# Pooled attention and a SiLU layer: the first batch's values loaded in two halves that are added by DMA, and its queries transposed earlier

## The chip, the cores and the metric

The kernel runs on one core of one Trainium2 chip. The metric is the device time of one execution in microseconds, the median of several runs. The profile is one execution taken by the hardware profiler; its times are counted from the start of its span. The engines are PE (TensorE: products, with PEld for its weight loads), DVE (VectorE), ACT (ScalarE), POOL (GpSimd) and SP (SyncE). DMA transfers are issued from the queues of POOL, SP and ACT and move on 16 DMA engines.

## The reference

```python
B, H, S, D = 8, 8, 576, 64           # batch, heads, sequence, head width
k_p = k.reshape(B, H, S // 8, 8, D).mean(axis=3)      # 72 pooled keys
v_p = v.reshape(B, H, S // 8, 8, D).mean(axis=3)      # 72 pooled values
scores = matmul(q, k_p.T) / sqrt(D)
attn = exp(scores - max) ; attn /= attn.sum(-1) + 1e-9
x = (attn @ v_p)  -> [B * S, H * D] = [4608, 512]
h = x @ w_in                          # 512 -> 2048
out = (h * sigmoid(h)) @ w_out        # 2048 -> 512, float32
```

Eight neighbouring keys, and eight neighbouring values, are averaged; attention runs against the 72 averages; its output goes through a layer with SiLU.

## The kernel before

The tokens go through the layer in nine tiles of 512 (t = 0 to 8), and attention of batch t + 1 is woven into tile t. Only batch 0 has nothing to hide behind: its attention is the head of the program.

In the head, keys and values are laid out with one group of eight rows (8 x 64 numbers) per partition: 576 groups make 4.5 slots of 128 partitions. A slot group is folded in three additions on VectorE (512 to 256 to 128 to 64 numbers per slot); products with a shifted identity ("select") then bring the sums into the order that attention needs.

```python
SLOTS, SA = 4, 3                       # four full slots and half a slot; tiles of 3 and 2 slots
RE = POOL * D                          # 512 numbers: eight rows

def load_slots(eng, b, name, i0, i1, half=None):
    es = slice(0, RE) if half is None else slice(half * RE // 2, (half + 1) * RE // 2)
    ...
    how = dict(accum_op=ALU.add) if half else {}      # half 1 is added to what half 0 left
    ...
    eng.dma_start(out=tiles[j][..., :w], in_=src[...], **how)

def slot_sums(name, j, halves=False):
    raw = row_tiles[name][j]
    dst = rows5[name][:, SA:] if j else rows5[name][:, :SA]
    w = RE // 4 if halves else RE // 2                # halves: one fold less
    while w > D:
        nc.vector.tensor_add(out=raw[..., :w], in0=raw[..., :w], in1=raw[..., w : 2 * w])
        w //= 2
    nc.vector.tensor_add(out=dst, in0=raw[..., :D], in1=raw[..., D : 2 * D])
```

`q_transpose(b, a, f)` is one VectorE transpose of a quarter of a batch's queries; `scores(b, g, f)` are eight products and four exponentials on ScalarE; `denominators` are four products and a reciprocal; `numerators(b, g, f)` are eight products with the pooled values and two multiplications on VectorE that write `xT`, the input of the layer. `warm_up(n)` issues n products whose result nobody uses.

The head of the program:

```python
    ... keys of batch 0 on the SP and ACT queues ...
    load_q(0, halves=True)
    load_q_half(0, 0)
    load_slots(nc.gpsimd, 0, "v", 0, 3)
    load_q_half(0, 1)
    load_slots(nc.gpsimd, 0, "v", 3, 4)
    load_slots(nc.gpsimd, 0, "v", 4, 5)
    attn_tables()
    nc.vector.memset(warm, 0.0)
    nc.vector.memset(ones, float(POOL))
    nc.gpsimd.memset(shifts, 0.0)
    make_identity(nc, ident, nomemset=True)
    # ... cut ...
    for c in range(3):
        load_w_in(512 * c, 512 * (c + 1))             # on the GpSimd queue, two transfers each

    warm_up(19)
    slot_sums("k", 0)
    select_k(0, 0)
    copy_k(0, 0, act_copy)
    warm_up(4)
    q_transpose(0, 0, 0)
    scores(0, 0, 0)
    slot_sums("k", 1)
    warm_up(3)
    select_k(0, 1)
    copy_k(0, 1, act_copy)
    q_transpose(0, 1, 0)
    warm_up(2)
    scores(0, 1, 0)
    denominators(0, 0, 0)
    slot_sums("v", 0)
    warm_up(2)
    select_v(0, 0, "mm")
    copy_v(0, 0, act_copy)
    denominators(0, 1, 0)
    q_transpose(0, 0, 1)
    scores(0, 0, 1)
    slot_sums("v", 1)
    warm_up(1)
    numerators(0, 0, 0, ("mm", "at"))
    warm_up(2)
    select_v(0, 1, "mm")
    copy_v(0, 1)
    q_transpose(0, 1, 1)
    warm_up(2)
    numerators(0, 1, 0, ("mm", "at"))
    scores(0, 1, 1)
    warm_up(2)
    ... keys, queries and values of batch 1, the last of w_in, and w_out on the GpSimd queue ...
    for t in range(NT):
        ...
        up(t, f_up, items)             # x @ w_in, SiLU
        ...                            # down: @ w_out
```

The first real products of the layer are those of `up(0, ...)`, line 518 of the kernel before; its first columns need both `numerators` groups of the head. Batch 2's keys and values are already loaded in halves by this kernel (`load_half_2`, during t = 0).

Of the kernel before, what the change touches and what calls it, by code (L numbers as in the profile page):

```python
# [36 lines left out]
def kernel(  # L37
# [9 lines left out]
    nc = tc.nc  # L47
# [185 lines left out]
    SLOTS = ROWS // 128  # L233
# [5 lines left out]
    SA = SLOTS - 1  # L239
# [10 lines left out]
    def load_slots(eng, b, name, i0, i1, half=None):  # L250
        es = slice(0, RE) if half is None else slice(half * RE // 2, (half + 1) * RE // 2)
        src = (k if name == "k" else v)[b].rearrange("h (sp p) d -> (h sp) (p d)", p=POOL)
        src = src[:, es]
        how = dict(accum_op=ALU.add) if half else {}
        tiles = row_tiles[name]
        w = es.stop - es.start
        if i0 == SLOTS:
            eng.dma_start(
                out=tiles[1][:REST, SLOTS - SA, :w], in_=src[128 * SLOTS :], **how
            )  # L260
        else:
            j = i0 // SA
            eng.dma_start(
                out=tiles[j][:, i0 - SA * j : i1 - SA * j, :w],
                in_=src[128 * i0 : 128 * i1].rearrange("(i r) e -> r i e", r=128), **how
            )

    def slot_sums(name, j, halves=False):
        raw = row_tiles[name][j]
        dst = rows5[name][:, SA:] if j else rows5[name][:, :SA]  # L270
        w = RE // 4 if halves else RE // 2
        while w > D:
            nc.vector.tensor_add(  # L273
                out=raw[..., :w], in0=raw[..., :w], in1=raw[..., w : 2 * w]
            )
            w //= 2
        nc.vector.tensor_add(out=dst, in0=raw[..., :D], in1=raw[..., D : 2 * D])
# [40 lines left out]
    def copy_v(b, a, copy=nc.vector.tensor_copy):  # L318
        hs = slice(4 * a, 4 * (a + 1))
        copy(out=batches[b]["vp"][:, hs, :], in_=batches[b]["v_ps"][:SP, hs, :])  # L320
# [3 lines left out]
    def scores(b, g, f):  # L324
        st = batches[b]
        sc = [ps_tile([128, 512], FP32, "at", "sc_ps")[:SP, :HS] for s in range(4)]
        for c in range(2):
            for s in range(4):
                rows = slice(32 * s, 32 * (s + 1))
                nc.tensor.matmul(  # L330
                    sc[s],
                    lhsT=kz[b % 2][rows, g, c, :],
                    rhs=st["qT"][rows, g, f * QF : (f + 1) * QF, c, :],
                    start=(c == 0), stop=(c == 1),
                )
        es = mid.tile([SP, 4, HS], BF16, tag="es", bufs=4, name="es")
        for s in range(4):
            nc.scalar.activation(es[:, s, :], sc[s], func=AF.Exp, scale=score_scale)  # L338
        st[f"es{g}{f}"] = es


    def denominators(b, g, f, on_dve=False):
        st = batches[b]
        es = st[f"es{g}{f}"]
        den_ps = ps_tile([128, 512], FP32, "at", "den_ps")
        for s in range(4):
            nc.tensor.matmul(  # L347
                den_ps[32 * s : 32 * (s + 1), :HS],
                lhsT=ones, rhs=es[:, s, :], start=True, stop=True,
            )  # L350
        rec = mid.tile([128, HS], FP32, tag="rec", bufs=4, name="rec")
        if on_dve:
            nc.vector.reciprocal(rec, den_ps[:, :HS])
        else:
            lnd = mid.tile([128, HS], FP32, tag="lnd", name="lnd")
            nc.scalar.activation(lnd, den_ps[:, :HS], func=AF.Ln)  # L356
            nc.scalar.activation(rec, lnd, func=AF.Exp, scale=-1.0)
        st[f"rec{g}{f}"] = rec
# [318 lines left out]
    load_slots(nc.sync, 0, "k", 4, 5)  # L677
    load_q(0, halves=True)
    load_q_half(0, 0)
    load_slots(nc.gpsimd, 0, "v", 0, 3)  # L680
    load_q_half(0, 1)
    load_slots(nc.gpsimd, 0, "v", 3, 4)
    load_slots(nc.gpsimd, 0, "v", 4, 5)
    attn_tables()
    nc.vector.memset(warm, 0.0)
    nc.vector.memset(ones, float(POOL))
# [12 lines left out]
    def load_w_out(c):  # L699
        cs = slice(c * KG // 4, (c + 1) * KG // 4)  # L700
        nc.gpsimd.dma_start(out=w_out_sb[:, cs, :], in_=w_out_r[:, cs, :])

    for c in range(3):
        load_w_in(512 * c, 512 * (c + 1))

# [12 lines left out]
    q_transpose(0, 1, 0)  # L718
    warm_up(2)
    scores(0, 1, 0)  # L720
    denominators(0, 0, 0)
    slot_sums("v", 0)
    warm_up(2)
    select_v(0, 0, "mm")
    copy_v(0, 0, act_copy)
    denominators(0, 1, 0)
    q_transpose(0, 0, 1)
    scores(0, 0, 1)
    slot_sums("v", 1)
    warm_up(1)  # L730
    numerators(0, 0, 0, ("mm", "at"))
    warm_up(2)
    select_v(0, 1, "mm")
    copy_v(0, 1)
    q_transpose(0, 1, 1)
    warm_up(2)
    numerators(0, 1, 0, ("mm", "at"))
    scores(0, 1, 1)
    warm_up(2)
# [8 lines left out]
    load_slots(nc.gpsimd, 1, "v", 3, 4)  # L748
    load_slots(nc.gpsimd, 1, "v", 4, 5)
    load_w_out(3)  # L750

    def load_half_2(name, half):
        for i0, i1 in ((0, SA), (SA, SLOTS), (SLOTS, SLOTS + 1)):
            load_slots(nc.gpsimd, 2, name, i0, i1, half)

    visits = [(f, g) for f in range(2) for g in range(2)]
    for t in range(NT):
# [42 lines left out]
        if a < B:  # L800
            q_at = [15, 16, 17, 49] if t > 1 else [24, 25, 26, 49] if t else [82, 84, 86, 88]
            if t == 0:
                for j in range(2):
                    f_up.append((44 + 8 * j, lambda j=j: slot_sums("k", j)))
                    f_up.append((72 + 8 * j, lambda j=j: select_k(1, j)))
                    f_up.append((72 + 8 * j, lambda j=j: copy_k(1, j)))
                    f_down.append((20 + 10 * j, lambda j=j: slot_sums("v", j)))
                    f_down.append((37 + 3 * j, lambda j=j: select_v(1, j, "at")))
                    f_down.append((37 + 3 * j, lambda j=j: copy_v(1, j)))
            elif t == 1:  # L810
                for j in range(2):
                    f_up.append((0, lambda j=j: slot_sums("k", j, halves=True)))
                    f_up.append((22, lambda j=j: select_k(2, j)))
                    f_up.append((23, lambda j=j: copy_k(2, j)))
                    f_down.append((8, lambda j=j: slot_sums("v", j, halves=True)))
                    f_down.append((40, lambda j=j: select_v(2, j, "at")))
                    f_down.append((41, lambda j=j: copy_v(2, j)))
            else:
                f_up.append((22, lambda: k_transpose(a)))
                f_down.append((10, lambda: pool_v(a)))  # L820
            for n in range(4):
                f_to = f_down if t and n == 3 else f_up
                f_to.append((q_at[n], lambda n=n: q_transpose(a, n // 2, n % 2)))
            if t == 0:
                f_down.append((0, lambda: load_half_2("k", 0)))
                f_down.append((0, lambda: load_q(2)))
                f_down.append((0, lambda: load_half_2("k", 1)))
                for half in range(2):
                    f_down.append((31, lambda half=half: load_half_2("v", half)))
                for y in range(2):  # L830
                    for n in U_W:
                        f_down.append((6, lambda y=y, n=n: unit_weight_sum(y, n)))
            elif a + 1 < B:
                for stage in range(2):
                    f_down.append((100, lambda stage=stage: pool_k(a + 1, stage)))
                f_up.append((0, lambda: load_q(a + 1)))
                f_up.append((1, lambda: load_one(a + 1, "k")))
                f_up.append((2, lambda: load_rest(a + 1, "k")))
                f_down.append((11, lambda: load_one(a + 1, "v")))
                f_down.append((12, lambda: load_rest(a + 1, "v")))  # L840
            f_down.append((0, attn_tables))

            if t:
                sc_at, den_at, nu_at = (1, 28, 56, 77), (28, 46, 69, 89), (46, 69, 89, 93)
            else:
                sc_at, den_at, nu_at = (1, 14, 22, 30), (14, 22, 30, 38), (42, 47, 52, 57)
            for n, (f, g) in enumerate(visits):
                f_down.append((den_at[n], lambda f=f, g=g: denominators(a, g, f)))
                f_down.append((sc_at[n], lambda f=f, g=g: scores(a, g, f)))


            for n, (f, g) in enumerate(visits):
                if n < 3 or not 3 <= t < B - 2:
                    at = nu_at[n] + 2 * (t == 1 and n == 0)
                    f_down.append((at, lambda f=f, g=g: numerators(a, g, f)))
                if n == 0 and 3 < t < B - 1:
                    f_down.append((nu_at[n], lambda: numerators(a - 1, 1, 1)))
# [34 lines left out]
```

The softmax here doesn't subtract the row's maximum and nothing guards it: scores larger than these inputs give would overflow.

## Time and profile before

| | |
|---|---|
| device time, median of 3 | 291.53 us (291.43 to 291.8) |
| span of the profiled execution | 288.6 us |
| granted TensorE clock | 0.998 |
| DMA | 37.67 MB, mean 131 GB/s |
| busy in the first 23 us: PE / DVE / ACT / POOL | 20.38 / 17.39 / 12.35 / 15.05 us |

A row of the timeline has the start in us, the duration in us, the engine, the line of the kernel, the operation with its output and input, and the count of merged instructions; a bracket gives how long the engine had been idle before and what it was waiting for. "PE busy" counts warm-up products too. A row of DMA issues has the count, the size and the microseconds from issue to landing. A row of the table by stretches has, after the engines, the granted clock, the DMA share and the GB/s moved.

### The profile page before, as it was taken

The numbers are of one execution on the slowest core, as the hardware profiler recorded it, in microseconds if no ns is written. First come the engines' busy times: TensorE is split into PE (matmuls) and PEld (weight loads), VectorE is DVE, ScalarE is ACT, GpSimd is POOL, SyncE is SP. The second block draws the span as 40 slices with busy tenths as digits, with TensorE's granted clock in tenths as the row PEclk, the third lists the DMA queues.
The fourth block names the chain that finished last, engine by engine and source line by source line (L and its number), as shares of the span: only waits on it lengthen the run. The fifth ranks groups of instructions, "written<-read, shape, count | busy, mean of one in ns | idle before, by whom it ended". The sixth has DMA issues, their size and how long they took to land.

```text
span 288.6 us, 6600 instructions
## 1 busy us (share of the span) xinstructions
PE 281.2 (97%) x2578; PEld 189.9 (66%) x2597; DVE 226.8 (79%) x417; ACT 187.9 (65%) x401; POOL 52.2 (18%) x68
## 2 busy tenths in 40 slices
PE   7989999999999999999999999999999999999995
PEld 2448434465667676657788767676777667786684
DVE  4986844989789796979698879887988876746783
ACT  1768675568656877578767866786679657425700
POOL 8744316501020011101200106203000000000000
PEclk9999999999999999999999999999999999999999
DMA  7999999893758565875995495979830023005004
GB/s 214 276 278 215 232 301 151 221 206 55 145 82 187 127 91 76 133 179 123 137 182 166 61 138 81 164 156 163 149 82 2 2 65 83 1 2 140 6 2 145
DMA packets 35295, 37.67 MB, mean 131 GB/s; under 512 B 9952, under 2 KB 27616, under 8 KB 35264
## 3 DMA queue, kind: packets, MB, share of 16 engines
q0 software_dynamic: 21760, 20.86, 43.3%
q1 hardware_dynamic: 12928, 15.48, 22.0%
q10 hardware_dynamic: 576, 0.92, 0.9%
q8 instruction: 20, 0.33, 0.5%
q14 instruction: 11, 0.09, 0.1%
HBM read 36.70 MB, written 9.44 MB: 160 GB/s over the span
## 4 chain that ended last, share of the span: by engine, by line
PE 91%; DVE 2%; ACT 2%; DMA 2%; issue 1%; DVEq 0%
PE hp_ps L518 24%; PE o_psP L623 15%; PE o_psQ L623 15%; PE u_psQ L460 6%; PE u_psP L460 6%; PE o_psR L623 5%; PE o_ps L550 4%; PE sc_ps L330 4%; PE nu_ps L370 3%; PE den_ps L347 3%; PE u_psR L460 2%; DMA raw<-in_k_dram 2%; PE warm_ps L672 1%; ACT es L338 1%; PE kz_ps L295 1%
## 5 line engine op out<-in xcount | busy, mean ns | idle before, releaser
L518 PE MATMUL hp_ps<-xT,w_in_sb 128*128 128x512 bf16 (+3 forms) x398 | 80.5, 338 | 1.2 <-ACT h_T L524 0.4
L524 ACT ACTIVATE h_T<-hp_ps 128x512 bf16<-128x512 f32 (+2 forms) x95 | 51.4, 545 | 33.1 <-PE hp_ps L518 31.9
L623 PEld LDWEIGHTS <-h_sum 128*128 128x128 bf16 x640 | 60.4, 98 | 15.2 <-issue 6.1
L583 DVE TENSOR_TENSOR h_sum<-h_T 128x1024 bf16<-128x1024 bf16 (+1 forms) x72 | 50.9, 743 | 7.0 <-ACT h_T L524 7.0
L518 PEld LDWEIGHTS <-w_in_sb 128*128 128x128 bf16 x412 | 39.3, 98 | 24.9 <-issue 1.5
L338 ACT ACTIVATE es<-sc_ps 72x288 bf16<-72x288 f32 x128 | 41.4, 402 | 12.6 <-PE sc_ps L330 12.5
L378 DVE TENSOR_TENSOR xT<-nu_ps,rec 128x288 bf16<-128x288 f32 x64 | 25.8, 450 | 13.2 <-PE nu_ps L370 13.0
L460 PEld LDWEIGHTS <-w_sum 128*128 128x128 bf16 x300 | 29.3, 98 | 7.7
L623 PEld LDWEIGHTS <-h_T 128*128 128x128 bf16 x256 | 23.5, 98 | 6.7 <-issue 4.3
L468 ACT ACTIVATE h_T<-c_sb 128x512 bf16<-128x512 f32 x30 | 18.8, 628 | 10.8 <-DVE c_sb L492 10.8
L152 DVE STREAM_TRANSPOSE qT<-q_bf 128x576 bf16<-128x576 bf16 x32 | 22.9, 753 | 0.0
L181 POOL DMA_DIRECT2D raw<-in_k_dram x5 | 7.0, 1405 | 75.1 <-DVE h_sum L583 37.7
L356 ACT ACTIVATE lnd<-den_ps 128x288 f32<-128x288 f32 x30 | 12.3, 411 | 10.8 <-PE nu_ps L370 5.8
L273 DVE TENSOR_TENSOR raw<-raw 128x384 f32<-128x384 f32 (+3 forms) x20 | 12.4, 619 | 8.0 <-DMA raw<-in_v_dram 4.4
L623 PE MATMUL o_psP<-w_out_sb,h_sum 128*128 128x256 bf16 x128 | 17.6, 273 | 0.0
L623 PE MATMUL o_psQ<-w_out_sb,h_sum 128*128 128x256 bf16 x128 | 17.6, 273 | 0.0
L623 PE MATMUL o_psQ<-w_sum,h_T 128*128 128x256 bf16 x128 | 17.5, 274 | 0.0
L623 PE MATMUL o_psP<-w_sum,h_sum 128*128 128x256 bf16 x128 | 17.0, 273 | 0.0
L623 PE MATMUL o_psR<-w_sum,h_sum 128*128 128x256 bf16 x128 | 16.7, 273 | 0.0
L623 PE MATMUL o_psP<-w_sum,h_T 128*128 128x256 bf16 x128 | 16.7, 273 | 0.0
L530 POOL DMA_DIRECT2D out_dram<-o_sb x1 | 0.6, 628 | 82.3 <-issue 82.3
L623 PE MATMUL o_psQ<-w_sum,h_sum 128*128 128x256 bf16 x128 | 15.4, 273 | 0.0
(77 smaller groups left out, 426.8 us busy)
## 6 DMA issues: line engine op xcount, KB each, us to landing
out_dram<-o_sb SPq DMA_DIRECT2D x128, 64.0 KB, 2.5
q_bf<-in_q_dram POOLq DMA_DIRECT2D x6, 576.0 KB, 11.4
raw<-in_k_dram SPq DMA_DIRECT2D x6, 512.0 KB, 5.5
raw<-in_k_dram POOLq DMA_DIRECT2D x5, 576.0 KB, 8.8
raw<-in_v_dram POOLq DMA_DIRECT2D x5, 576.0 KB, 8.7
raw<-in_v_dram SPq DMA_DIRECT2D x5, 512.0 KB, 6.4
w_in_sb<-in_moe_w_in_dram POOLq DMA_DIRECT2D x8, 256.0 KB, 8.7
w_out_sb<-in_moe_w_out_dram POOLq DMA_DIRECT2D x4, 512.0 KB, 13.5
```

Source lines behind the costliest of these rows:

```text
L152: nc.vector.transpose(out=st["qT"][:, a, f * QF : (f + 1) * QF].rearrange("r i c p -> r (i c p)"), in_=st["q_bf"][:, a, f * n : (f + 1) * n],)
L273: nc.vector.tensor_add(out=raw[..., :w], in0=raw[..., :w], in1=raw[..., w : 2 * w])
L330: nc.tensor.matmul(sc[s], lhsT=kz[b % 2][rows, g, c, :], rhs=st["qT"][rows, g, f * QF : (f + 1) * QF, c, :], start=(c == 0), stop=(c == 1),)
L338: nc.scalar.activation(es[:, s, :], sc[s], func=AF.Exp, scale=score_scale)
L356: nc.scalar.activation(lnd, den_ps[:, :HS], func=AF.Ln)
L378: nc.vector.tensor_mul(out=xT[:, 2 * g + c, cols], in0=nu[c][:, :HS], in1=rec)
L460: nc.tensor.matmul(ps[bank][:, u, :], lhsT=w[:, kk, 128 * u : 128 * (u + 1)], rhs=x[:, kk, :], start=first and u == 0 and kk == 0, stop=kk ...
L468: nc.scalar.activation(h_T[:, g : g + 2, j * NQ : (j + 1) * NQ], src, func=AF.Silu)
L518: nc.tensor.matmul(hp_ps[:, r0:r1], lhsT=w_in_sb[:, kk, g * 128 : (g + 1) * 128], rhs=xT[:, kk, x0 : x0 + r1 - r0], start=(kk == 0), stop= ...
L524: nc.scalar.activation(h_T[:, g, n0 : n0 + n], hp_ps[:, :n], func=AF.Silu)
L583: nc.vector.tensor_tensor(out=h_sum[n][:, ks, :], in0=quarter(*a, ks), in1=quarter(*b, ks), op=op)
L623: nc.tensor.matmul(ps[b][:, c, :], lhsT=left(n, kt, c), rhs=W_OUT[n][:, kt, :], start=b not in begun, stop=kt == k1 - 1, skip_group_check= ...
```

## The change

Batch 0's values no longer come as 512 numbers per slot. The first 256 numbers of every slot are loaded, and the second 256 are added to them by the transfer itself (`accum_op=ALU.add`), so that VectorE has one fold less to do. The second half of the transfers goes into GpSimd's queue after the queries and ahead of the layer's weights. All four transposes of batch 0's queries now stand ahead of the value sums, the value sums and selects are done together, and both copies of the pooled values are on VectorE. The helper `load_half_2` is renamed `load_half` and takes the batch.

```diff
+    def load_half(b, name, half):
+        for i0, i1 in ((0, SA), (SA, SLOTS), (SLOTS, SLOTS + 1)):
+            load_slots(nc.gpsimd, b, name, i0, i1, half)
 ...
     load_q_half(0, 0)
-    load_slots(nc.gpsimd, 0, "v", 0, 3)
+    load_half(0, "v", 0)
     load_q_half(0, 1)
-    load_slots(nc.gpsimd, 0, "v", 3, 4)
-    load_slots(nc.gpsimd, 0, "v", 4, 5)
 ...
+    load_half(0, "v", 1)
     for c in range(3):
         load_w_in(512 * c, 512 * (c + 1))
 ...
     scores(0, 1, 0)
+    for a in range(2):
+        q_transpose(0, a, 1)
     denominators(0, 0, 0)
-    slot_sums("v", 0)
+    warm_up(3)
+    scores(0, 0, 1)
+    denominators(0, 1, 0)
+    for j in range(2):
+        slot_sums("v", j, halves=True)
+    warm_up(3)
+    for a in range(2):
+        select_v(0, a, "mm")
+    for a in range(2):
+        copy_v(0, a)
     warm_up(2)
-    select_v(0, 0, "mm")
-    copy_v(0, 0, act_copy)
-    denominators(0, 1, 0)
-    q_transpose(0, 0, 1)
-    scores(0, 0, 1)
-    slot_sums("v", 1)
-    warm_up(1)
     numerators(0, 0, 0, ("mm", "at"))
-    warm_up(2)
-    select_v(0, 1, "mm")
-    copy_v(0, 1)
-    q_transpose(0, 1, 1)
-    warm_up(2)
     numerators(0, 1, 0, ("mm", "at"))
     scores(0, 1, 1)
     warm_up(2)
```

The instructions after the head are the same in the same order on every engine.

More of the change, by code (lines that the diff above doesn't have):

```diff
@@ L750 @@
     load_w_out(3)
-    def load_half_2(name, half):
-        for i0, i1 in ((0, SA), (SA, SLOTS), (SLOTS, SLOTS + 1)):
-            load_slots(nc.gpsimd, 2, name, i0, i1, half)
     visits = [(f, g) for f in range(2) for g in range(2)]
@@ L824 @@
             if t == 0:
-                f_down.append((0, lambda: load_half_2("k", 0)))
+                f_down.append((0, lambda: load_half(2, "k", 0)))
                 f_down.append((0, lambda: load_q(2)))
-                f_down.append((0, lambda: load_half_2("k", 1)))
+                f_down.append((0, lambda: load_half(2, "k", 1)))
                 for half in range(2):
-                    f_down.append((31, lambda half=half: load_half_2("v", half)))
+                    f_down.append((31, lambda half=half: load_half(2, "v", half)))
                 for y in range(2):
```

## The prediction

> **What bounds the kernel now.** I began with the page: how busy each engine is, then the chain that ended last, then the timeline of the head and of the first pass over the hidden layer.
>
> ```profile
> PE 281.2 (97%) x2578; PEld 189.9 (66%) x2597; DVE 226.8 (79%) x417; ACT 187.9 (65%) x401; POOL 52.2 (18%) x68
> ...
> PE 91%; DVE 2%; ACT 2%; DMA 2%; issue 1%; DVEq 0%
> ```
>
> TensorE is 91% of the chain, so what counts is the moment at which real matmuls start, and whether they stop again. The change touches only the head. The timeline of the head:
>
> ```profile
> 9.15 0.77 DVE L152 STREAM_TRANSPOSE qT<-q_bf 128x576 bf16<-128x576 bf16 x1
> 9.84 1.51 DVE L273 TENSOR_TENSOR raw<-raw 128x768 f32<-128x768 f32 x2
> 11.39 0.36 DVE L277 TENSOR_TENSOR v<-raw 128x192 bf16<-128x192 f32 x1
> 11.66 0.77 DVE L152 STREAM_TRANSPOSE qT<-q_bf 128x576 bf16<-128x576 bf16 x1
> 12.60 1.15 DVE L273 TENSOR_TENSOR raw<-raw 128x512 f32<-128x512 f32 x2 [0.16 <-DMA raw<-in_v_dram]
> 13.79 0.29 DVE L277 TENSOR_TENSOR v<-raw 128x128 bf16<-128x128 f32 x1
> ...
> 15.07 0.42 DVE L320 CAST vp<-v_ps 72x256 bf16<-72x256 f32 x1 [0.26 <-PE v_ps L313]
> ...
> 16.10 0.78 DVE L378 TENSOR_TENSOR xT<-nu_ps,rec 128x288 bf16<-128x288 f32 x2
> ...
> 17.05 0.41 PE L518 MATMUL hp_ps<-xT,w_in_sb 128*128 128x288 bf16 x2
> ```
>
> From 5.24 us, when the first keys have landed, to 16.88 us VectorE is hardly idle: the bracket in the row at 12.60 is 0.16 us, the one at 15.07 is 0.26 us. TensorE fills its waits with warm-up products until the first real product at 17.05 (L518). So the head is bound by VectorE, and what ends the head is a fixed tail behind the last value sum, which ends at 13.79 + 0.29 = 14.08: select, copy, numerators, two multiplications by the reciprocals; the real products begin 17.05 - 14.08 = 2.97 us later.
>
> The other thing to read is how full the transfers are. The mean DMA share is 0.99 to 1.25 in every microsecond from 3 to 23, and GpSimd's transfers land in the order of their issue. The times to landing, by issue:
>
> ```profile
> raw<-in_v_dram POOLq DMA_DIRECT2D x1, 768.0 KB, 7.2
> ```
>
> ```profile
> raw<-in_v_dram POOLq DMA_DIRECT2D x1, 256.0 KB, 7.6
> ```
>
> The first three value slots are issued at 2.50 and land at 9.7; the fourth is issued at 4.35 and lands at 11.95; the last, issued at 4.88, lands at 12.5. The first query pair lands at 6.97 and 7.47 (issue 1.27 and 1.97, 5.7 and 5.5 us), the second at 10.4 and 11.1.
>
> **What the Trainium skill says.** "VectorE: DVE Perf Modes", Mode 2x_2P, says that fp32 tensor_tensor stays at one result a cycle; the trace agrees, as the 768-wide fp32 addition takes 959 ns and the 384-wide one 558. So taking the widest fold off VectorE saves real time. "DMA: Bandwidth & Descriptors", section SWDGE vs HWDGE vs iDMA, says that accumulation during a transfer is for GpSimd's queue only, where software writes the descriptors; its Rules for kernel authors say that an accumulating transfer reads its destination and writes it later, so that the earlier transfer's semaphore must be waited for first. The trace agrees: in batch 2 the accumulating half is issued at 44.35 after 6.23 us of waiting on the plain half. "TensorE: Matmul & The Clock Gate", Part 1, says the array falls to half clock after an idle window of about 3.4 us; here the first warm-up products took 0.43 us each and the later ones 0.21 to 0.24, so a long gap in the head could cost something.
>
> **What an accumulating half costs here.** The kernel already loads batch 2 this way. The issue and the time to landing of the first piece (384 KB) of its keys, and then the transfers' share in two stretches, one when the accumulating half moves and one when the plain half behind it does:
>
> ```profile
> 44.35 1.32 POOL L263 DMA_DIRECT2D raw<-in_k_dram  x1 [6.23 <-DMA raw<-in_k_dram]
> ```
>
> ```profile
> raw<-in_k_dram POOLq DMA_DIRECT2D x1, 384.0 KB, 5.2
> ```
>
> ```profile
> 48.00:49.00 1.00, 1.00 (x12) 0.32 (x10) 0.82 (x3) 0.58 (x2) 1.00 (x3) 1.00 1.23 195
> ...
> 52.00:53.00 1.00, 1.00 (x12) 0.41 (x5) 1.00 (x4) 0.00 (x0) 0.00 (x0) 1.00 0.99 373
> ```
>
> The last two columns are DMA share and GB/s. The accumulating half moves some 190 GB/s with the engines full, the plain one some 370: twice the time for the same bytes. And 5.2 us to landing although nothing was queued ahead: the rate climbs to its level only about 2.2 us after the issue. The second and third piece land at 50.35 and 50.65, that is 6.0 and 6.3 us after the first issue. The values of batch 2 repeat it: first piece 5.3 us.
>
> **The change, part by part.**
>
> *Removed from VectorE.* The 768-wide (0.96 us) and the 512-wide (0.68 us) fold of the values. Ahead of the last value sum it would free 1.6 us. One copy of the pooled values goes from ScalarE (0.35 us) to VectorE (0.42 us). The four transposes are the same number, moved: the two of the second query half now stand ahead of the value sums. If the values lay ready, VectorE would have after 9.92: transposes 2 x 0.77, sums 0.56 + 0.36 + 0.42 + 0.29, copies 0.84, products 1.60, ending near 15.6 instead of 16.88. That is the most this can give, 1.3 us.
>
> *Arrival of the plain half.* It has 0.59 MB: 393 KB, 131 KB and 66 KB. The first piece starts when the query pair is in, 7.47, and at 350 GB/s (the old 786 KB took 2.2 us, so 357) needs 1.1 us: 8.6. Then 9.0 and 9.2. The second query half follows: 10.0 and 10.7 (its two pieces took 0.7 us each).
>
> *Issue of the accumulating half.* GpSimd must wait for the first piece: 8.6 + 0.25 (44.35 is 0.3 us after the piece it adds to had landed, 30.04 + 14.0) = 8.85. In batch 2 the next two issues follow 0.8 and 1.4 us later: 9.65 and 10.25.
>
> *Arrival of the accumulating half.* 8.85 + 5.2 = 14.05 for the first piece, 14.9 and 15.1 for the others. A second way of working: 8.85 + 2.2 until bytes move, 0.59 MB at 190 GB/s = 3.1, and some 0.8 for the receipt, gives 15.0. The queries have moved before 11.05, so there is also a hole of about 1 us in the transfers.
>
> *VectorE after that.* First sum pair 14.05 to 14.97, second pair from 15.1: 0.42 + 0.29, ends at 15.8. The old last sum ended at 14.08. The tail is nearly the same length: the second select's six products end 0.5 us later, copy to 1.1 us, two numerator groups to 1.8 us, scores and two warm-up products to about 2.75 us, and the multiplications to 3.1 us, against 2.97 before. So real products begin **1.7 us later**.
>
> *Given back.* Before, TensorE waited 0.41 us at 19.77 for ScalarE, which had exponentials (1.30) and a table load (1.28) right ahead of the first activation. The exponentials now come earlier relative to the real products, by some 0.3 us, so I take back 0.3 us: **+1.4 us**.
>
> *Later transfers.* The first layer's weights now stand behind the accumulating half. The last value piece was in at 12.5 and will be at 15.1, so everything behind comes 2.6 us later, while TensorE comes 1.5 us later: slack shrinks by about 1.1 us. Slack before: first weight chunk 17.05 - 14.75 = 2.3; keys of batch 1, sums ended at 26.73 for a select at 28.57, 1.8; the last weight chunk landed at 29.5 (issue 18.80 plus 10.7) for products at about 31.2 (29.14, seven of 0.11 us and six of 0.22), 1.7; first output weights 32.05 for 34.14, 2.1. All stay above zero by 0.6 us or more, so I add only 0.1 us for stalls. The rest of the program is the same instructions in the same order, and so shifts as a whole. Sum: 291.5 + 1.4 + 0.1 = **293.0 us**.
>
> **The rivals.**
> *A: the values come early enough.* If the first piece were in by 12.6 and the last by 13.4, the sums would end at 14.1 and nothing changes; earlier still, up to 1.3 us is won: 290.2 to 291.5. For it: the plain half is smaller than the old first load. Against it: the 5.2 and 5.3 us measured twice, with nothing queued ahead.
> *B: the weights become the bound.* If the accumulating transfers cost the queue more than 2.6 us (the third piece of batch 2's values landed 7.6 us after the first issue, not 6.3), the chunk for the last first-layer columns arrives after TensorE wants it, or the keys of batch 1 do: 294 to 295.5. For it: transfers are full from 3 us on.
> *C: the clock.* TensorE has about 1.5 us without work before the select; a drop of the clock there would cost a microsecond or two. Against it: the gap is less than half the window, and warm-up products stand around it.
>
> **Range and chances.** My step is +1.5; rival A has perhaps 15%, B 15%, C 5%. 8 times in 10 between 291.3 and 294.6. 2% is 5.8 us, more than the whole head could give or take by any of these: faster 0.01, same 0.97, slower 0.02.
>
> **What would show it.** VectorE idle 2 to 3 us ahead of the first value sum, waiting on the value transfer; first piece of the accumulating half issued near 8.9 and landing near 14.0; last value sum ending near 15.8; first real product near 18.7; no waits of TensorE on weights afterwards; a gap after the head that stays constant to the end. It is wrong if the last value sum ends before 14.1, if the head is later by 1.7 us and the end is not, or if the first pass shows new idle time of TensorE on weights.

## The result, and the profile after

The changed kernel takes 296.13 us (median of four executions, 295.82 to 297.6) against 291.48 us for the kernel before beside it: ratio 1.0159, 95% interval 1.0118 to 1.02. It is slower by 4.6 us, three times the loss that was predicted (1.5 us) and outside the range. The profiled execution, 297.6 us, is the slowest of the four, with a span of 295.8 us; its head may show the loss somewhat larger than a usual execution has it.

The first lines of the page, and its chain that ended last, by engine:

```profile
PE 286.0 (97%) x2598; PEld 190.7 (64%) x2598; DVE 225.9 (76%) x416; ACT 187.8 (64%) x400; POOL 54.9 (19%) x71
...
PE 89%; DMA 5%; DVE 2%; issue 1%; POOL 1%; ACT 1%; DVEq 0%; POOLq 0%
```

In the chain, DMA has gone from 2% to 5% of the span and TensorE from 91% to 89%. The page's list of lines names it: the values' transfer, 5%. The head in the timeline:

```profile
9.79 2.25 POOL L263 DMA_DIRECT2D raw<-in_v_dram  x2 [2.97 <-DMA raw<-in_v_dram]
...
14.80 0.56 DVE L277 TENSOR_TENSOR raw<-raw 128x384 f32<-128x384 f32 x1 [2.74 <-DMA raw<-in_v_dram]
...
15.80 0.43 PE L317 MATMUL v_ps<-v,shifts 128*72 128x64 bf16 x8 [1.48 <-DVE v L281]
...
18.21 0.43 DVE L277 TENSOR_TENSOR raw<-raw 128x256 f32<-128x256 f32 x1 [2.46 <-DMA raw<-in_v_dram]
...
18.67 0.29 DVE L281 TENSOR_TENSOR v<-raw 128x128 bf16<-128x128 f32 x1
...
23.26 0.69 PE L522 MATMUL hp_ps<-xT,w_in_sb 128*128 128x288 bf16 x2
```

GpSimd waits 2.97 us for the plain half before it may issue the accumulating one at 9.79. VectorE then waits 2.74 us and once more 2.46 us for values, where the kernel before had brackets of 0.16 and 0.26 us. The last value sum ends at 18.67 + 0.29 = 18.96 instead of 14.08, and the first real products (L522, line 518 before) begin at 23.26 instead of 17.05 and take 0.69 us for two instead of 0.41. Of the 6.2 us, 4.9 are the later sum and 1.3 a longer tail behind it (4.30 for 2.97 us).

The longer tail goes with the clock: in e1 below, which has the same order of instructions and keeps the full clock, the tail is 3.05 us. In the changed kernel's trace the granted clock is half from 18.36 to 25.18 and full on both sides of that; a stretch at one granted clock is called a stage here. The table by stretches, cut at 18.36 and in steps of 3.41 us from it (after the stretch: its length, then PE, PEld, DVE, ACT, POOL busy, the granted clock, DMA share, GB/s):

```profile
11.53:14.95 3.42, 2.77 (x26) 1.02 (x23) 0.68 (x2) 3.34 (x11) 3.42 (x7) 1.00 0.90 139
14.95:18.36 3.41, 0.43 (x8) 0.35 (x8) 0.92 (x3) 0.63 (x2) 1.40 (x3) 1.00 0.81 116
18.36:21.77 3.41, 2.76 (x25) 1.05 (x25) 2.10 (x7) 0.00 (x0) 2.29 (x4) 0.50 1.23 196
21.77:25.18 3.41, 3.41 (x20) 1.12 (x16) 1.59 (x4) 2.79 (x6) 1.77 (x3) 0.50 1.22 234
```

In 14.95 to 18.36 TensorE is busy for 0.43 us of 3.41; the two stretches that follow run at half clock.

Last the chain of the stage 0 to 27 us, followed back from its end (start, length, what):

```profile
2.50 7.00 DMA raw<-in_v_dram
...
9.79 0.15 POOL raw L263
...
11.17 6.94 DMA raw<-in_v_dram
...
18.21 0.44 DVE raw L277
...
19.01 0.53 PE v_ps L317 x4
```

Two transfers of 7.00 and 6.94 us stand in it one behind the other, from 2.50 to 18.12, with 1.67 us between them in which GpSimd issues the second half. No fold, transpose or score of the head is in it before 18.2.

### The profile page after: what moved, and what is told of

The parts are those of the page before. It is cut to its first block, busy times and chain, and to the rows that moved or that the text cites. A ratio compares the mean times of both kernels' runs of the same rounds, so it can differ in the third digit from the quotient of the medians.

```text
span 295.8 us, 6623 instructions
## 1 busy us (share of the span) xinstructions
PE 286.0 (97%) x2598; PEld 190.7 (64%) x2598; DVE 225.9 (76%) x416; ACT 187.8 (64%) x400; POOL 54.9 (19%) x71
## 3 DMA queue, kind: packets, MB, share of 16 engines
HBM read 36.70 MB, written 9.44 MB: 156 GB/s over the span
## 4 chain that ended last, share of the span: by engine, by line
PE 89%; DMA 5%; DVE 2%; issue 1%; POOL 1%; ACT 1%; DVEq 0%; POOLq 0%
PE hp_ps L522 24%; PE o_psP L627 15%; PE o_psQ L627 15%; PE u_psQ L464 6%; PE u_psP L464 6%; PE o_ps L554 5%; PE o_psR L627 5%; DMA raw<-in_v_dram 5%; PE sc_ps L334 4%; PE nu_ps L374 3%; PE den_ps L351 2%; PE u_psR L464 2%; DVE rr_sb L484 1%; DVE c_sb L496 1%; PE warm_ps L676 1%
## 5 line engine op out<-in xcount | busy, mean ns | idle before, releaser
L522 PE MATMUL hp_ps<-xT,w_in_sb 128*128 128x512 bf16 (+3 forms) x412 | 83.1, 342 | 0.0
L522 PEld LDWEIGHTS <-w_in_sb 128*128 128x128 bf16 x412 | 39.5, 98 | 24.9 <-issue 1.7
L277 DVE TENSOR_TENSOR raw<-raw 128x384 f32<-128x384 f32 (+3 forms) x18 | 10.8, 597 | 12.6 <-DMA raw<-in_v_dram 9.1
L554 PE MATMUL o_ps<-w_out_sb,h_T 128*128 128x512 bf16 x64 | 15.9, 381 | 0.0
```

Of the source, the lines that this page charges most:

```text
L522: nc.tensor.matmul(hp_ps[:, r0:r1], lhsT=w_in_sb[:, kk, g * 128 : (g + 1) * 128], rhs=xT[:, kk, x0 : x0 + r1 - r0], start=(kk == 0), stop= ...
L554: nc.tensor.matmul(ps, lhsT=h_T[:, g, m * 128 : (m + 1) * 128], rhs=w_out_sb[:, g, :], start=(g == 0), stop=(g == KG - 1),)
```

## The experiments

The theory after the result: the two value loads in series are the new bound of the head, and the fold that they take off VectorE was not on the path of the kernel before. The rivals: the new order of the instructions costs it; the half rows or the number of transfers cost it; the clock costs it. The indented text of an experiment says what was expected before it ran. Changes in us below are the ratio's distance from 1 times 291.2 us, the kernel before; brackets behind a ratio are its 95% interval.

**e1. The new order alone.** The changed kernel with values loaded whole and folded as before.

```diff
-    load_half(0, "v", 0)
+    load_slots(nc.gpsimd, 0, "v", 0, 3)
     load_q_half(0, 1)
+    load_slots(nc.gpsimd, 0, "v", 3, 4)
+    load_slots(nc.gpsimd, 0, "v", 4, 5)
-    load_half(0, "v", 1)
-        slot_sums("v", j, halves=True)
+        slot_sums("v", j)
```

> The new order of the head with the values loaded whole, as before. If the accumulating transfers are the cause (theory), the order alone costs nothing: VectorE has the same work, the last value sum ends near 15.6 us instead of 14.1 because two transposes stand ahead of it, but the tail after it is shorter by one transpose; 291 to 292 us. If the order is the cause (rival), it is as slow as the changed kernel, 295 to 296 us.

Measured: 292.35 us, ratio 1.0051 (1.0026 to 1.0076), +1.5 us. In its trace the last value sum ends at 15.08 and the first real product is at 18.13, 1.0 and 1.1 us later than before. The order itself costs: two transposes of 0.7 us now stand ahead of the value sums, and the chain of this head runs through both:

```profile
10.32 1.55 DVE qT L152 x2
11.87 0.85 DVE raw L277
...
14.79 0.30 DVE v L281
```

So the new order puts the value sums on the path. A part of the 1.5 us is the clock: 4 of the 14 executions have a mean granted clock of 0.988 to 0.994 and take 292.8 to 294.5 us; the median of the other ten is 291.8.

**e2. The halves alone.** The kernel before, in its own order, with the two half loads and the shorter sums.

```diff
-    load_slots(nc.gpsimd, 0, "v", 0, 3)
+    load_half(0, "v", 0)
 ...
+    load_half(0, "v", 1)
 ...
-    slot_sums("v", 0)
+    slot_sums("v", 0, halves=True)
```

> The values in two halves, the second added by the transfer, in the old order of the head. Theory: VectorE's queue now stands behind the values with a transpose still after them, so at least as slow as the changed kernel, 295.5 to 297.5 us. If the order is the cause (rival): 291 to 293 us.

Measured: 296.33 us, ratio 1.0173 (1.0144 to 1.0201), +5.0 us. The halves alone cost as much as the whole change; the two costs don't add, because in both kernels the head waits for the values.

**e3. No fall of the clock.** The changed kernel with more unused products ahead of the selects.

```diff
-    warm_up(3)
-    for a in range(2):
-        select_v(0, a, "mm")
+    warm_up(12)
+    select_v(0, 0, "mm")
+    warm_up(8)
+    select_v(0, 1, "mm")
```

> The changed kernel with warm-up products through the wait for the values (12 instead of 3 ahead of the first select, 8 between the two). Theory: the late arrival is about two thirds of the loss and the half clock after the wait the rest; with the clock kept, 1 to 2 us come back, 294 to 295 us. If the clock is most of the loss (rival): 292 us or less. If it is nothing: 296 us.

Measured: 295.66 us, ratio 1.0183 (1.0129 to 1.0236); the clock is 1.0 throughout the profiled execution (one of the four, 298.9 us, had 0.989; the others lie within 0.2 us of 295.6). The tail from the last value sum (17.02) to the first real product (20.83) is 3.8 us, the added products included. Yet the median falls by only 0.5 us, and the ratio not at all. The first pass over the hidden layer, from its first product to the first output product, takes 18.4 us for 17.1 before. In its timeline the keys of batch 1 are late:

```profile
29.75 1.55 DVE L277 TENSOR_TENSOR raw<-raw 128x768 f32<-128x768 f32 x2 [3.05 <-DMA raw<-in_k_dram]
...
33.35 0.64 PE L299 MATMUL kz_ps<-shifts,k 128*32 128x72 bf16 x12 [0.45 <-DVE kz L306]
```

VectorE waits 3.05 us for these keys, and TensorE's selects wait for VectorE, 0.20 and 0.45 us; that accounts for about half of the 1.3 us by which the pass is longer. It looks as if two bounds lay close behind one another: what the clock loses in the changed kernel, the late keys take in part if the clock doesn't.

**e4. The second half without wait or addition, new order.** It lands beside the first half and is not added: the values' sum lacks it. All bytes still move.

```diff
-    load_half(0, "v", 1)
+    load_beside()          # plain, into the other 256 numbers of each row
```

> The second half is loaded beside the first as a plain transfer, in the same place of the queue, and is not added to anything: same bytes, same number of transfers, VectorE's work as in the changed kernel, without accumulation and without the wait for the first half. It leaves out the sum of the second half, so its output lacks half of batch 0's values. Theory: the last piece lands near 12.8 us, real products begin at 16 to 16.5, 290.3 to 291 us. If the splitting into small transfers or their place in the queue is the cause (rival): 294 us or more.

Measured: 292.11 us, ratio 1.0046 (1.0022 to 1.0071). The last piece landed at 12.71, the last value sum ended at 12.98; the first real product is at 17.05, where the kernel before has it. With values a whole microsecond earlier than there, the head gains nothing. Against e1, which has the same order, the first real product comes 1.1 us earlier: in that order the values count. What e4 still loses lies behind the head: its first output product is at 35.13 for 34.14 before, with waits of TensorE of 0.45 us on the keys of batch 1 and 0.15 on weights that the kernel before does not have.

**e5. The same in the old order.** Again the second half is left out of the sum.

> The second half of the values loaded beside the first, plain and not added (half of batch 0's values is left out), in the OLD order of the head. If one fold less on VectorE is worth something once the data are there (theory), real products begin near 15.5 to 16 us, 1 to 1.5 us ahead of the kernel before; the time falls by less, since the weights and the keys of batch 1 come no earlier: 290.2 to 291.2 us. If the transfers behind it are the next bound (rival): the first output product starts no earlier than before (34.1 us) and the time is 291 us or more.

Its edit is e4's on the kernel of e2. Measured: 291.89 us, ratio 1.0017 (0.9999 to 1.0034). The last value sum ended at 12.10, 2.0 us earlier than before, with a fold less: no gain. (Its first real product is at 17.96; the head began late, as in e12 below.) Half rows and three more transfers alone cost at most 1 us.

**e6. The wait without the addition.** The changed kernel, the second half overwriting the first: the same wait and the same bytes, but a plain transfer (the first half is lost from the sum).

```diff
-        how = dict(accum_op=ALU.add) if half else {}
+        how = dict(accum_op=ALU.add) if half and not over else {}
 ...
-    load_half(0, "v", 1)
+    load_half(0, "v", 1, over=True)
```

> The changed kernel, but the second half overwrites the first instead of being added to it (the first half is left out of the result): same wait for the first half, same places in the queue, same bytes, no accumulation. If the accumulation itself is slow (theory): a plain piece has its first bytes earlier and moves at twice the rate, the last piece lands 2 to 3 us earlier than in the changed kernel, near 12.5 to 13.5 us, and the time is 292 to 293 us. If the wait for the first half is the cost (rival): lands near 15, 295 us or more.

Measured: 294.08 us, ratio 1.0096 (1.0073 to 1.0118), +2.8 us. It still issues only after a wait of 2.64 us, but the landing comes earlier:

```profile
9.01 1.48 POOL L263 DMA_DIRECT2D raw<-in_v_dram  x2 [2.64 <-DMA raw<-in_v_dram]
...
14.74 0.43 DVE L277 TENSOR_TENSOR raw<-raw 128x256 f32<-128x256 f32 x1 [1.23 <-DMA raw<-in_v_dram]
```

The first piece landed 3.5 us after its issue (12.54) instead of 5.0 in the changed kernel. With the ratios of e1, e4, e6 and the changed kernel this makes a ladder: new order +1.5, half rows unadded on top +1.3 in all, with the wait +2.8, with the addition +4.6. The wait is thus worth about 1.5 us and the addition about 1.8; the intervals of these two steps (0.5 to 2.4 and 0.5 to 3.2 us, the two ratios' half widths added in squares) exclude zero. Each step counts all that it brings about further on, such as a clock that falls or, in e6, 0.77 us of waiting for weights at 34.06.

**e7. Cheaper values without a second load.** The kernel before, batch 0's values cast to bf16 by the load, whole, and folded in bf16 (the sums are rounded more).

```diff
-    load_slots(nc.gpsimd, 0, "v", 0, 3)
+    load_slots(nc.gpsimd, 0, "v0", 0, 3)      # v0: a bf16 tile
 ...
-    slot_sums("v", 0)
+    slot_sums("v0", 0)
```

> The kernel before, with one change of another kind for the same aim: batch 0's values are loaded whole and cast to bf16 by the transfer, so that VectorE folds bf16 instead of fp32. No second transfer and no wait. Theory: the two large folds take about half (0.96 to 0.5 us, 0.68 to 0.36), VectorE saves 1 to 1.4 us ahead of the last value sum, real products begin near 16 us and the time is 290 to 291 us. Rival (the next bound is the transfers): 291 us or more.

Measured: 291.31 us, ratio 1.0008 (0.9996 to 1.0021). Folds that are cheaper on VectorE bring nothing that can be told from zero either.

**e8. Fill the hole in the transfers.** The changed kernel with the first two weight transfers ahead of the accumulating half, to use the 1 us in which nothing moves.

```diff
+    load_w_in(0, 512)
     load_half(0, "v", 1)
-    for c in range(3):
+    for c in range(1, 3):
```

> The changed kernel with the first two transfers of the layer's weights put ahead of the accumulating half, where the transfers stood idle for about 1.5 us. Theory: the hole is filled, the last value piece lands about 1 to 1.5 us later than in the changed kernel, the weights and the keys of batch 1 come about 1.5 us earlier; the head is later, so 296 to 298 us. If the lateness of what is queued behind is the main cost (rival): 294 to 295 us.

Measured: 297.58 us, ratio 1.0215 (1.0178 to 1.0251). The hole is filled (a DMA share of 1.23 and 1.24 from 10 to 12 us, where the changed kernel has 0.46 and 0.09), and the accumulating half comes later still: its last sum ends at 19.43 for 18.96. The hole was a sign of the serial wait, not a loss in itself.

**e9. A better order.** On e7's values: each select as soon as its sum is there, the late transposes between the value sums, fewer warm-up products.

```diff
     slot_sums("v0", 0)
-    warm_up(2)
+    q_transpose(0, 0, 1)
+    warm_up(1)
     select_v(0, 0, "mm")
-    copy_v(0, 0, act_copy)
+    copy_v(0, 0)
+    q_transpose(0, 1, 1)
     denominators(0, 1, 0)
-    q_transpose(0, 0, 1)
     scores(0, 0, 1)
 ...
-    warm_up(2)
     select_v(0, 1, "mm")
     copy_v(0, 1)
-    q_transpose(0, 1, 1)
-    warm_up(2)
+    warm_up(1)
     numerators(0, 1, 0, ("mm", "at"))
     scores(0, 1, 1)
-    warm_up(2)
```

> A version meant to beat both: values of batch 0 whole and cast to bf16 by the load, the two late query transposes between the value sums and not behind the last copy, both numerator groups ahead of the last scores, five warm-up products fewer between the last key scores and the layer. Theory (the head's chain is keys, then TensorE's and ScalarE's order with the last transpose and the exponentials behind it): ScalarE's last exponentials start about 1.2 us earlier, real products begin near 15.7 to 16.2 us, 290 to 290.6 us, faster than both by 0.2 to 0.4%. If the values' folds on VectorE bound the head (rival): no gain beyond the kernel with bf16 values, 291.3 us.

Measured: 290.44 us, ratio 0.9977 (0.9962 to 0.9992), faster than both kernels. Its timeline:

```profile
15.81 0.42 PE L521 MATMUL hp_ps<-xT,w_in_sb 128*128 128x288 bf16 x2
...
18.98 0.41 PE L521 MATMUL hp_ps<-xT,w_in_sb 128*128 128x288 bf16 x2 [0.60 <-ACT h_T L527]
```

Real products begin 1.24 us earlier than before, though the last value sum ends at 13.92, almost where it was. Part is lost again at 18.98, to ScalarE's exponentials and its table ahead of the first activation. Its chain runs through the value sums from 13.02 to 13.83, so the cheaper folds may have a share in it; this order with float32 values was not run. The fewer warm-up products seem to have a price: in 5 of its 22 executions the mean granted clock was 0.988, with times of 291.7 to 293.3 us, while all 59 executions of the kernel before beside it had 0.998 or more.

**e10. Six transfers of whole rows.** Late landing behind the halves: their rows of 1 KB, or the number of transfers? The kernel before with its values in six pieces of whole 2 KB rows.

```diff
-    load_slots(nc.gpsimd, 0, "v", 0, 3)
+    for i in range(3):
+        load_slots(nc.gpsimd, 0, "v", i, i + 1)
 ...                                   # slot 3 in two pieces of 64 partitions, then the rest
```

> The kernel before with the values in six transfers instead of three, all with whole rows of 2 KB (three single slots, then the fourth slot in two halves of partitions, then the last). Same head, same work. If rows of 1 KB make the transfers behind them uneven (theory), they stay even here: last key piece of batch 1 landed by 24.5 us, time 291 to 291.5 us. If the number of transfers does (rival): it lands at 26 us or later, 291.7 us or more.

Measured: 293.79 us, ratio 1.0071 (1.0044 to 1.0098). It answers another question than the one asked: the further issues stand ahead of the identity on GpSimd, which is done at 9.02 us instead of 6.35, and the first key select waits for it until 9.07.

**e11. Without the keys' widest fold.** The kernel before with the second half of each key row left out of the sum; all loads stay.

```diff
-    slot_sums("k", 0)
+    slot_sums("k", 0, halves=True)
 ...
-    slot_sums("k", 1)
+    slot_sums("k", 1, halves=True)
```

> The kernel before without the widest fold of batch 0's KEYS (half of each key's rows is left out; loads unchanged). It takes 0.96 + 0.68 us of VectorE out ahead of the two key selects. Theory (the keys lead the head's chain): real products begin about 1 us earlier, at 16 us, 290 to 290.7 us. If the head is bound by the order behind it (rival): nothing, 291.2 us.

Measured: 290.82 us, ratio 0.9991 (0.9978 to 1.0004). The keys' first sum ends at 6.21 instead of 7.18, but the first select comes at 7.20, behind the warm-up products in TensorE's order.

**e12. Without the values' widest fold.** The same for the values: what the change wanted to win, at no cost.

```diff
-    slot_sums("v", 0)
+    slot_sums("v", 0, halves=True)
 ...
-    slot_sums("v", 1)
+    slot_sums("v", 1, halves=True)
```

> The kernel before without the widest fold of batch 0's VALUES (half of each value's rows is left out; loads unchanged): what the change wanted to take off VectorE, at no price at all. If VectorE bounds the head, as the prediction said: real products begin 1.3 us earlier, 290.2 us. If the value folds lie beside the chain (theory now): real products begin at the same time within 0.1 us, 291.2 us.

Measured: 291.11 us, ratio 0.999 (0.9978 to 1.0001): a gain of at most 0.6 us. The time from the first exponential of the head to the first real product is 8.16 us, as in the kernel before (8.17). In this execution the head began 0.8 us late; the beginning of its chain shows why:

```profile
1.20 6.88 PE warm_ps L672 x19
8.08 0.21 PE kz_ps L295 x8
```

The warm-up products, most of them at half clock, lasted until 8.08. The keys' first sum had been ready at 7.20.

**e13. Six whole-row transfers, the second three behind the identity.**

```diff
-    load_slots(nc.gpsimd, 0, "v", 0, 3)
+    for i in range(3):
+        load_slots(nc.gpsimd, 0, "v", i, i + 1)
 ...
     make_identity(nc, ident, nomemset=True)
 ...                                   # slot 3 in two pieces and the rest: here
```

> The kernel before, with batch 0's values in six plain transfers of whole 2 KB rows, the second three issued behind the identity's instructions on GpSimd (in e10 they stood ahead of it and held the first key select until 9.07 us). Theory A, the late landing behind the halves comes from their 1 KB rows: the last keys of batch 1 land by 24.6 us as in the kernel before (24.42), the 16 engines of a later transfer end within 2 us of each other, 291.2 to 291.6 us. Theory B, it comes from the number of transfers: last keys of batch 1 at 25.5 us or later, the 16 engines spread by 2.3 us or more, 291.8 to 293.8 us.

Measured: 291.42 us, ratio 1.0003 (0.9995 to 1.0012). By the time, the number of transfers costs nothing. By the trace it is not so clean: the last keys of batch 1 landed at 25.14, and the 16 completion marks of one later transfer lie 1.7 to 2.4 us apart. That is between the kernel before (24.42) and e4 and e5 with half rows (26.77 and 26.43; marks up to 3.3 us apart). The profiled execution was this kernel's slowest, 294.02 us. Whether the number of transfers has a share beside the short rows, and how much each has, is left open.

**e14. Fewer warm-up products.** The kernel before with 14 for 19.

```diff
-    warm_up(19)
+    warm_up(14)
```

> The kernel before with 14 warm-up products for 19 ahead of the first key select. Theory: the warm-up products hold the first key select in the executions where the full clock comes up late (8.01 to 8.16 us in e5 and e12 against 7.2 otherwise), so with five fewer the first select follows the keys' sum at 7.2 to 7.4 us whenever the clock comes, 291.0 to 291.3 us and less scatter. Rival: the warm-up products are what brings the clock up, so that with fewer of them it comes later and the selects and transposes run at half speed, 291.5 to 292.5 us.

Measured: 290.82 us, ratio 0.9986 (0.9977 to 0.9996). In the profiled execution the full clock came only at 7.21, and still the first select is at 7.27, where warm-up products and the keys' first sum end within 0.1 us of each other:

```profile
1.20 6.14 PE warm_ps L672 x14
7.34 0.21 PE kz_ps L295 x8
```

With 19 of them, e5 and e12 had their first select at 8.16 and 8.01, in executions with a late clock. So the warm-up products do hold the head there, and five fewer bring 0.4 us (0.1 to 0.7). The scatter did not shrink: 290.37 to 291.94 us, against 290.56 to 292.12 for the kernel before.

**e15. Both together.** e9 with 14 warm-up products.

> e9 with 14 warm-up products for its 19. Theory that the head's chain is TensorE's own order from the first key select on: nothing lost against e9, 290.0 to 290.5 us, ratio 0.996 to 0.998. Rival, colder clock: 290.8 us or more.

Measured: 290.14 us, ratio 0.9963 (0.9948 to 0.9978): the fastest version, 1.1 us below the kernel before; six executions do not tell it apart from e9.

## Why the prediction was wrong, step by step

*"The head is bound by VectorE": this step failed.* VectorE is busy there, but its value folds lie beside the path. The end of the kernel before's chain, taken from 0 to 20 us:

```profile
12.75 0.42 PE sc_ps L330 x8
...
13.80 0.31 PE nu_ps L370 x4
14.11 0.54 PE warm_ps L672 x2
14.65 0.33 PE v_ps L313 x6
...
15.07 0.42 DVE vp L320
15.49 0.70 DVE qT L152
...
16.23 0.48 PE sc_ps L330 x8
16.71 1.29 ACT es L338 x4
...
18.02 1.28 ACT L386
```

No value fold is in it, here or earlier; the folds that it has, from 5.24 to 7.20, are those of the first keys. The second select (14.65) follows two warm-up products in TensorE's order, not the value sum that ended at 14.08; then come the copy, the last query transpose, scores, exponentials and ScalarE's table. The prediction measured a "fixed tail of 2.97 us behind the last value sum" where there were two events that happened to be that far apart. e12, e5 and e4 show it: last sums at 13.58, 12.10 and 12.98, which is 3.9, 2.3 and 4.0 us behind the first exponential for 5.2 before, and yet first exponential to first product at 8.16, 8.15 and 8.09 us, against 8.17 before. So the change had nothing to win through the fold, not "1.3 us". The margin is narrow, about half a microsecond between the value sum and the second select; in e11, where the last value piece landed at 12.82 and its sum ended at 14.39, the chain does run through the value sums.

*The new order.* The prediction took the order as free and counted only its gain. e1 measures it at +1.5 us (0.8 to 2.2), with the value sums now on the path.

*Plain half, "8.6", "9.0", "9.2".* 8.67, 9.12 and 9.44 in e2's trace; 9.49, 9.91 and 10.15 in the changed kernel's, where the keys ahead of it landed about 0.5 us later too. The first piece, issued at 2.50 in all of them, landed between 8.67 and 9.84 in e2, e3, e4, e5, e6, e8 and the changed kernel: the prediction stands at the early edge.

*Issue of the accumulating half, "8.85".* 8.97 in e2, 9.46 in e3, 9.79 in the changed kernel, always about 0.3 us behind the landing. The mechanism was right.

*Its landing, "5.2 us after".* First piece: 5.0 us in the changed kernel, 5.2 in e2. Right, as is the hole: the DMA share was 0.09 between 11 and 12 us. The last piece was the mis-sized term: predicted 15.1, it was 15.62 and 16.18 in e2 and e3, and 18.12 in the changed kernel. There nine of the 16 completion marks of the second and of the third piece had come by 15.73 and 16.08, the last only at 17.91 and 18.12; why some of the engines lagged is not settled.

*The sum for the last value sum.* Predicted 15.8, measured 18.96: 0.94 us from the later issue, 2.08 from the last piece (18.12 - 9.79 = 8.33 us for the predicted 6.25), 0.14 from the sums. In e2, whose first piece was issued nearly when predicted, it was 16.51.

*The tail, "3.1 us".* 4.30 us. In e1, with the same order and the full clock, it is 3.05. The 1.25 us between are rival C, the clock, given 5%. The argument against it, a gap of less than half the window, failed twice: in the changed kernel TensorE stood still for 1.48 and 2.77 us around one select, and in e6 no gap was longer than 1.40 us and the clock fell all the same. The Trainium skill, "TensorE: Matmul & The Clock Gate", Part 1, calls the window free-running: it is not reset when a kernel starts. The traces agree with that: each full-clock stage from the warm-up on, and each half-clock stage behind it in the head, is a whole multiple of 3.41 us long (13.65 and 6.83 in the changed kernel, 10.24 and 10.24 in e2, 13.65 and 3.41 in e6), and the first of them begins anywhere from 4.03 (e9) to 7.21 us (e14). What went with the fall in these heads is little work of TensorE in one fixed window. The last window at full clock in e6 and one in e1, which kept the clock:

```profile
14.54:17.95 3.41, 2.10 (x30) 0.83 (x29) 2.52 (x7) 0.59 (x2) 3.01 (x6) 1.00 1.06 150
```

```profile
12.20:15.61 3.41, 2.59 (x29) 1.48 (x29) 2.77 (x7) 3.09 (x10) 2.52 (x4) 1.00 1.23 199
```

2.10 us of work in it and the clock fell, as it did after 0.43 us in the changed kernel and 0.25 in e2; 2.59 us and it stayed. A few warm-up products "around the gap" do not help if one window is left with too little. But the busy time of the trace is not the whole rule: at the end of e14 a window with less work than that of e6, in wider products, kept the clock.

```profile
283.69:287.10 3.41, 1.62 (x15) 1.21 (x13) 1.19 (x3) 0.00 (x0) 0.63 (x1) 1.00 0.46 154
```

What exactly is counted stays open. The windows lie differently in each execution, and in e1 and e9 some executions keep the clock and others lose it; that the one is the reason for the other is not shown.

*"Given back 0.3".* The wait of TensorE on ScalarE after the head (0.41 us before) is indeed gone in the changed kernel, where the last exponentials start 0.90 us ahead of the first real product for 0.35 before. But that is TensorE at half clock in between. In e1, the same order at full clock, they start 0.42 us ahead and the wait is 0.33: the order gives back 0.1 us, not 0.3.

*Later transfers, "slack stays above 0.6, stalls 0.1".* In the changed kernel's trace no wait of TensorE is listed after 23 us; it is itself later than the data. In e3 it is earlier and does wait for the keys of batch 1: rival B in its second form, put at 15%. The last of these keys landed at 24.42 before, and at 30.57 in the changed kernel: 6.2 us later, not "2.6".

*The time.* +1.4 in the head became +6.2 in the profiled execution, whose span grew by 7.2 us (the first output product is 6.5 us later), and +4.6 in the median. The range held the three rivals one at a time; here the new order, the late last piece, the clock and, close behind, the late keys came together. The wait and the slow addition, 1.5 and 1.8 us, are the larger part, and the rest of the 4.6 is in the order and the half rows.

## What to carry to other kernels

Before work is taken off an engine, follow the chain of that stage back and see whether the work is in it; a full busy column and a constant distance between two events say nothing about which waits for which. Ask it again for the new order: e1 put on the path what had been beside it. A load that must wait for another load costs its whole latency again (here 7.0 and 6.9 us in series), so look for adding in DMA where both loads are hidden: behind batch 2's, the trace of the kernel before shows no wait of TensorE. In a head without other work, look at TensorE's work in every stretch of 3.41 us and not only at its longest gap, and don't put more warm-up products ahead of the first real one than the data's arrival covers.

## What the runs showed of the hardware that was not expected

- The accumulating transfers are slow to move as well as to issue: with the engines full they moved 197 GB/s (changed kernel, 13 to 14 us), the plain ones of e6 397 (11 to 12 us). The issue instructions on GpSimd took 1.31, 1.46 and 1.71 us, plain ones of the same shapes 0.77, 0.57 and 0.54 us in e6, and the plain weight issues behind them 1.0 to 1.8 us instead of 0.71.
- Behind half-row transfers the 16 DMA engines lie further apart: the completion marks of one later transfer (weights and keys of batch 1) are 2.4 to 3.6 us apart in the changed kernel, at most 1.9 us in the kernel before and 2.1 in e1, both with whole rows. All of a transfer has to land, so each counts as late as its slowest engine: VectorE's last sum in the changed kernel began at 18.21, behind the last mark of 18.12, though nine of the 16 had come by 16.08. e13 leaves open how much of this is the rows.
- To come back from half clock a window had to be nearly full: 2.76 us of work in 3.41 was not enough in the changed kernel, nor were 3.18 and 3.09 in e2, while 3.09 was in e6, and 3.41 was in the changed kernel and in e2. Under the warm-up products at the start, 2.85 us were enough in the kernel before and 2.59 were not in e14. The busy time alone does not give a sharp limit.
